# Pooled attention with a two-expert adapter: all gated activations of chunks 10 to 67 turned by DMA, in pairs

## The chip, the cores and the metric

The kernel runs on one core of one Trainium2 chip. The metric is the device time of one launch in microseconds (us). The kernel before was run three times: 378.42, 378.78 and 379.87, so its median is 378.78. Besides the five engines (PE for matrix products, DVE and ACT for elementwise work, POOL for more of it, SP for issuing transfers) the core has 16 DMA engines, which move data and can transpose 16-bit data on the way.

## The reference

`N` is 12288 queries for each of four batches, `C` is 128. Keys and values are the same 768 rows: 4 x 4 patches of `kv`, averaged and multiplied by `w_sr`. The attention output goes into a mixture of adapters with 8 experts of rank 16, of which the two with the largest logits count for each row.

```python
kv_pool = kv.reshape(B, H // r, r, W // r, r, C).mean(axis=(2, 4))
k = v = kv_pool.reshape(B, -1, C) @ w_sr
s = (q @ k.transpose(0, 2, 1)) / np.sqrt(C)
a = np.exp(s - s.max(-1, keepdims=True))
a /= a.sum(-1, keepdims=True) + 1e-09
x = (a @ v).reshape(B * N, C)                      # 49152 rows

logits = x @ w_gate
topk = the two largest of the 8 logits of each row
w = softmax over these two
out = x + sum over the two experts e of  w_e * (x @ A[e]) @ B[e]
```

## The kernel before, in words

The 49152 rows are 96 chunks of 512; a chunk is four tiles of 128 rows (`S` = 4). The main loop (line 588) has one slot per chunk, from slot 8 to slot 95; an order written out by hand (`opening`) stands in front of it and a tail behind it. Instructions run on each engine in the order in which the program gives them, and `keep` holds to that order.

In slot k, PE works on several chunks at once, each at another step:

- `unit()` three times (`scores`): two matmuls of 512 columns each give the scores of chunk k against a third of the keys, in one of two PSUM buffers (`ps_s`, tile `sg`); ACT writes their exponentials to `em`.
- `attend`, 24 matmuls: exponentials of chunk k-1 times the values (`acc`). The values carry a column of ones and seven differences of router logits, so that the sums and the logits come out of the same product.
- `normalize` (DVE, start of slot k, for chunk k-2): `xn` = `acc` / sum. `xn` tiles are a ring of six, two chunks to a tile. `top` (DVE) and `route`, `gates` (POOL, and a tanh on ACT) make the expert weights `gw`, two chunks at a time up to chunk 67.
- `transposes` (line 381): four PE transposes of `xn` of chunk k-4, and for some chunks four more of `hg` (below) of chunk k-5, into one PSUM tile `tt_ps`. One DVE copy brings it to SBUF (`tts`).
- `down` (line 427, chunk k-4): four matmuls with all experts' `A`, to `h_ps`. `gate` (line 432, DVE): `hg` = `h_ps` x `gw`, in bf16.
- `hg` must be transposed once more. For even chunks up to 60, and for 62 to 67, PE does this a slot later, within `transposes`. For odd chunks from 9 to 61 (`by_queue`, line 542) the gate writes to a tile `hs`, and `turn_h_dma` (line 422) has SP issue a DMA that transposes it into a tile `ht`.
- `up` (line 441): four matmuls with all experts' `B`, to `d_ps`; `finish` (line 450): DVE adds `xn` and writes `osb`, which SP stores. This comes two slots after the chunk's `down` where PE has transposed, six slots after it where the DMA has (`late_up`, line 677).

`tt_ps`, `d_ps` and `h_ps` take turns in two PSUM buffers (`ps_m`, tag `mb`). In the code of a slot the order is: first score unit, `transposes`, second unit (line 653), `up`, a quarter of `attend`, third unit, `down`, the other quarters.

From slot 72 on (chunks 68 to 89, `by_dma`) another branch of the loop runs (line 604): there both `xn` and `hg` are transposed by DMA, in tiles named `turn`, one transfer for both in a slot, and the order is first unit, `down`, second unit, `gate`, transfer, `up`, half of `attend`, third unit, the other half.

SP issues transfers in the order of the program: the stores, the loads of `kv` rows for the next batches (`load_kv`), the transposes, and `load_qT`, which loads 2048 queries by a transposing DMA from a bf16 copy in DRAM. `load_qT` stands in the slots of `loads` (line 481): every fourth slot from 10 to 62, and 57, 59, 61, 64, 65 and 66. In a slot with an odd chunk's DMA transpose it stands behind that transpose, otherwise at the start of the slot. POOL issues the casts to that copy.

Of the kernel before, what the change touches and what calls it, by code (L numbers as in the profile page):

```python
# [10 lines left out]
FP32 = mybir.dt.float32  # L11
BF16 = mybir.dt.bfloat16
# [8 lines left out]
def kernel(  # L21
# [10 lines left out]
    nc = tc.nc  # L32
    P = 128
    B, N, C = q.tensor.shape
# [5 lines left out]
    S = T // P  # L40
# [17 lines left out]
    gpool = ctx.enter_context(tc.tile_pool(name="gpool", bufs=6))  # L58
    run = ctx.enter_context(tc.tile_pool(name="run", bufs=3))
    hpool = ctx.enter_context(tc.tile_pool(name="hpool", bufs=4))  # L60
    opool = ctx.enter_context(tc.tile_pool(name="opool", bufs=8))
    qdram = ctx.enter_context(tc.tile_pool(name="qdram", bufs=1, space=bass.MemoryType.DRAM))
    ps_s = ctx.enter_context(tc.tile_pool(name="ps_s", bufs=2, space=bass.MemoryType.PSUM))
    ps_a = ctx.enter_context(tc.tile_pool(name="ps_a", bufs=1, space=bass.MemoryType.PSUM))
# [2 lines left out]
    keep = tc.keep_in_program_order  # L67
# [41 lines left out]
    q_f = {}  # L109

    def load_q(g, m):
        q_f[g, m] = opool.tile([P, S, C], FP32, tag="osb", name="qf")
        src = q[0, g * GT:(g + 1) * GT].rearrange("(p j) c -> p j c", p=P)
        keep(nc.sync.dma_start(q_f[g, m], src[:, m * S:(m + 1) * S]))

# [220 lines left out]
    SOLO, TURN = NCHUNK - 6, NCHUNK - 28  # L336
# [82 lines left out]
        for i, (d, k) in enumerate(what):  # L419
            d[k] = strip(t, 1)[:, lo + i]  # L420

    def turn_h_dma(k):
        hgT[k] = hpool.tile([P, S, P], BF16, tag="ht", name="ht", bufs=5)
        keep(nc.sync.dma_start(hgT[k].rearrange("c s p -> c s p"),
                               hg[k].rearrange("p s c -> p (s c)"), transpose=True))

    def down(k):
        hp[k] = mtile([P, S, P], name="h_ps")
# [3 lines left out]
    def gate(k, into=None):  # L432
        k0, m = first[k], k - first[k]
        hg[k] = run.tile([P, S, P], BF16, tag="hg", name="hg") if into is None else into
        keep(nc.vector.tensor_tensor(  # L435
            hg[k].rearrange("p s (e r) -> p (s e) r", e=E),
            hp[k].rearrange("p s (e r) -> p (s e) r", e=E),
            gw[k0][:, m * S:(m + 1) * S].rearrange("p s e -> p (s e)")
            .unsqueeze(2).broadcast_to([P, S * E, RK]), op=ALU.mult))
# [10 lines left out]
    def finish(k):  # L450
        osb = opool.tile([P, S, C], FP32, tag="osb", name="osb")
        keep(nc.vector.tensor_tensor(osb, dp[k], xn[k][:, :, 0:C], op=ALU.add))  # L452
        store(nc.sync, k, osb)
        for d in (em, acc, xn, xT, hgT, hp, hg, dp):
            d.pop(k, None)
# [19 lines left out]
    def unit(k=None, r=None):  # L475
        k, r = units.pop(0 if k is None else units.index((k, r)))
        scores(k, r)
# [61 lines left out]
        left = [k for k in left if k not in enter[t]]  # L539
        t += 1  # L540

    by_queue = [k for t in range(13, TURN - 2) for k in enter[t] if k % 2]
    late_up = {}

    kh, ku, kd, kdone = [], [], [], []
    engines = {"DVE": nc.vector, "ACT": nc.scalar, "POOL": nc.gpsimd}
# [41 lines left out]
    for k in range(k1, NCHUNK):  # L588
        b, i = divmod(k, NB)
        ka = att.get(k, [])  # L590
        kx = enter.get(k, [])
        begin(k, False)

        def after_norm(kn):
            top(kn)
            if kn == first[kn] + size[kn] - 1:
                route(first[kn])

        kn = [n for n in att.get(k - 1, []) if normed[n] == k]
        unit()  # L600
        if k in loads and not any(x_ in by_queue for x_ in kx):
            load_qT(loads[k])
        ku = ku + late_up.pop(k, [])
        if kx and not kd and all(x_ in by_dma for x_ in kx):
            down(kx[0])
            todo = []
            for n in kn:
                normalize(n)
                if n in by_dma:
                    narrow(n, k)  # L610
                    todo = [(xT, n)]
            tanhs()
            for h_ in kh:
                if h_ not in by_dma:
                    transposes(None, h_, nc.vector)
            unit()
            gate(kx[0], strip(k, 0)[:, 1])
            todo.append((hgT, kx[0]))
            if len(kx) == 1:
                turn_dma(k, *todo)  # L620
            for u_ in ku:
                up(u_)
                finish(u_)
            attend(ka[0], 0)
            attend(ka[0], 1)
            unit()
            for n in kn:
                after_norm(n)
            attend(ka[0], 2)
            for x_ in kx[1:]:  # L630
                down(x_)
                gate(x_, strip(k, 0)[:, 0])
                turn_dma(k, (hgT, x_), *todo)
            attend(ka[0], 3)
            kh, ku = kx, [c for c in kh if c not in by_queue]
            continue
        tanhs()
        for x_ in kd:
            down(x_)
        for n in kn:  # L640
            normalize(n)
            if n in by_dma:
                narrow(n, k)
                turn_dma(k, (xT, n))
        px = [c for c in kx if c not in by_dma]
        ph = [c for c in kh if c not in by_dma and c not in by_queue]
        pairs = [(px[j] if j < len(px) else None, ph[j] if j < len(ph) else None)
                 for j in range(max(len(px), len(ph)))]
        for x_, h_ in pairs[:1]:
            transposes(x_, h_, nc.vector)  # L650
        for x_ in kd:
            gate(x_)
        unit()
        for u_ in ku:
            up(u_)
            finish(u_)
        for a_ in ka[:-1]:
            for s in range(S):
                attend(a_, s)
            normalize(a_)  # L660
            after_norm(a_)
        if ka and len(ka) == 1:
            attend(ka[0], 0)
        for n in kn:
            after_norm(n)
        if k >= 13:
            unit()
            n0 = 1
        else:
            attend(ka[0], 1)  # L670
            n0 = 2
        for x_ in kx[:1]:
            down(x_)
            if x_ in by_queue:
                gate(x_, hpool.tile([P, S, P], BF16, tag="hs", name="hs"))
                turn_h_dma(x_)
                late_up[k + 6] = [x_]
                if k in loads:
                    load_qT(loads[k])
            else:  # L680
                gate(x_)
        kd = []
        if rest and i in ((14, 15, 16, 18, 19, 20, 21, 22, 23) if b == 0 else (5, 6, 7, 13, 14, 15, 21, 22, 23)):
            rest.pop(0)()
        for a_ in ka[-1:]:
            for s in range(n0 if len(ka) == 1 else 0, S):
                if s == S - 1:
                    for x_, h_ in pairs[1:]:
                        transposes(x_, h_, nc.scalar)
                        kd = [x_] if x_ is not None else []  # L690
                attend(a_, s)
        ku = [c for c in kh if c not in by_queue]
        kh = kx[:1] + kdone
        kdone = kd
        if k % 2 == 0 and 8 <= k <= 20:
            for _ in range(4 if k == 18 else 3):
                sums.pop(0)()
        for w in adds_at.get(k, []):
            add_patches(*w)
# [181 lines left out]
```

## Time and profile before

| | |
|---|---|
| median of the runs | 378.78 us (378.42 to 379.87) |
| the profiled execution | 378.59 us, of which the span from the first to the last instruction is 376.8 |
| stores of 256 KB | 94, median 4.0 us from issue to landing |
| DMA transposes into `ht` | 27, median 6.6 us |
| DMA transposes of the `turn` tiles | 23, median 3.1 us |
| query loads into `qT` | 18, median 8.1 us |

The profile is of one execution. The rows that the prediction quotes come from these views: the page (span, busy time of each engine, chain of waits); groups by tile (count, shortest, median and longest duration in ns, first and last start in us); the timeline (start in us, length in us, engine, line, operation, out<-in, count; in brackets the engine's idle time before, and who ended it); the waits of SP's queue (us in total, times, longest); and windows (for each engine busy us and instructions, then the granted clock of TensorE, the busy share of the 16 DMA engines and GB/s). L70 is a helper that issues all matmuls, so these are told apart by their tiles. The lengths of matmuls are modelled, their starts are recorded.

### The profile page before, as it was taken

The numbers are of one execution on the slowest core, as the hardware profiler recorded it, in microseconds if no ns is written. First come the engines' busy times: TensorE is split into PE (matmuls) and PEld (weight loads), VectorE is DVE, ScalarE is ACT, GpSimd is POOL, SyncE is SP. The second block draws the span as 40 slices with busy tenths as digits, with TensorE's granted clock in tenths as the row PEclk, the third lists the DMA queues.
The fourth block names the chain that finished last, engine by engine and source line by source line (L and its number), as shares of the span: only waits on it lengthen the run. The fifth ranks groups of instructions, "written<-read, shape, count | busy, mean of one in ns | idle before, by whom it ended". The sixth has DMA issues, their size and how long they took to land.

```text
span 376.8 us, 11335 instructions
## 1 busy us (share of the span) xinstructions
PE 365.9 (97%) x4340; PEld 287.5 (76%) x4340; DVE 300.5 (80%) x925; ACT 293.6 (78%) x368; POOL 218.2 (58%) x493
## 2 busy tenths in 40 slices
PE   8899999999999999999999999999999999999993
PEld 5667788877788787877877787787877777777782
DVE  1446799888888888888888888898898777777785
ACT  1548986787878788788878868877878999999873
POOL 0120368888766566557557566755645666666452
PEclk9999999999999999999999999999999999999997
DMA  8979669999999999999999999999875686777523
GB/s 255 397 261 218 231 176 271 298 268 255 240 288 265 185 288 312 182 241 294 240 259 249 287 275 203 204 257 243 211 211 156 169 170 170 169 151 186 143 88 139
DMA packets 66311, 85.75 MB, mean 228 GB/s; under 512 B 42736, under 2 KB 43504, under 8 KB 65904
## 3 DMA queue, kind: packets, MB, share of 16 engines
q1 hardware_dynamic: 62656, 73.29, 70.0%
q0 software_dynamic: 3168, 11.54, 18.2%
q8 instruction: 34, 0.56, 0.6%
q10 hardware_dynamic: 432, 0.20, 0.2%
q14 instruction: 21, 0.17, 0.2%
HBM read 50.53 MB, written 36.70 MB: 232 GB/s over the span
## 4 chain that ended last, share of the span: by engine, by line
PE 88%; DMA 6%; DVE 3%; ACT 1%; issue 1%; POOL 0%; SPq 0%; ACTq 0%; POOLq 0%
PE acc L70 35%; PE sg L70 32%; PE tt_ps L70 6%; PE d_ps L70 5%; PE h_ps L70 5%; DMA kvr<-in_kv_dram 4%; DMA qf<-in_q_dram 2%; PE v_ps L70 1%; PE kpT_ps L70 1%; DVE xn L330 1%; DVE tts L399 1%; DMA out_dram<-osb 1%; ACT em L304 1%; PE kfT_ps L70 0%; PE tail_ps L70 0%
## 5 line engine op out<-in xcount | busy, mean ns | idle before, releaser
L304 ACT ACTIVATE em<-sg 128x1024 f16<-128x1024 f32 x288 | 282.7, 1022 | 64.7 <-PE sg L70 62.0
L70 PE MATMUL acc<-vx,em 128*128 128x136 f16 x2280 | 166.5, 223 | 0.0
L70 PEld LDWEIGHTS <-em 128*128 128x128 f16 x2304 | 145.3, 98 | 8.2 <-DVE xn L330 0.6
L70 PE MATMUL sg<-qT,kfT 128*128 128x512 bf16 x480 | 142.0, 379 | 0.8 <-ACT em L304 0.7
L330 DVE TENSOR_TENSOR xn<-acc,rinv 128x540 f32<-128x540 f32 x95 | 68.4, 720 | 3.3
L452 DVE TENSOR_TENSOR osb<-d_ps,xn 128x512 f32<-128x512 f32 x91 | 62.4, 688 | 1.1
L362 POOL TENSOR_TENSOR over<-xn,srt 128x64 f32<-128x64 f32 (+1 forms) x120 | 30.9, 278 | 50.5 <-DVE srt L350 50.4
L502 POOL TENSOR_TENSOR kvr<-kvr 128x512 f32<-128x512 f32 (+1 forms) x48 | 56.9, 1201 | 0.5
L70 PEld LDWEIGHTS <-tts 128*128 128x128 bf16 x456 | 34.6, 97 | 25.4 <-issue 0.4
L70 PEld LDWEIGHTS <-kfT 128*128 128x128 bf16 x576 | 46.3, 98 | 4.5 <-issue 1.0
L377 POOL TENSOR_TENSOR gw<-th,over 128x64 f32<-128x64 f32 (+1 forms) x60 | 17.3, 289 | 51.7 <-ACT th L375 49.6
L325 DVE RECIPROCAL rinv<-acc 128x4 f32<-128x4 f32 x95 | 17.3, 182 | 36.1 <-PE acc L70 35.2
L399 DVE COPY tts<-tt_ps 128x1024 bf16<-128x1024 bf16 (+1 forms) x73 | 41.6, 569 | 0.0
L435 DVE TENSOR_TENSOR hg<-h_ps,gw 128x512 bf16<-128x512 f32 x44 | 30.4, 691 | 9.1 <-POOL gw L378 8.4
L70 PEld LDWEIGHTS <-xn 128*128 128x128 bf16 x296 | 22.6, 98 | 16.7 <-DVE xn L330 0.4
L350 DVE MAX8 srt<-xn 128x8 f32<-128x8 f32 x380 | 34.5, 153 | 0.1
L70 PE MATMUL sg<-qTs,kfT 128*128 128x512 bf16 x96 | 28.6, 379 | 0.0
L70 PE MATMUL tt_ps<-id_bf,xn 128*128 128x128 bf16 x284 | 27.4, 219 | 0.0
L70 PE MATMUL h_ps<-a_bf,tts 128*128 128x128 bf16 x284 | 27.4, 219 | 0.0
L368 POOL TENSOR_SCALAR over<-over 128x64 f32<-128x64 f32 (+1 forms) x60 | 19.8, 331 | 5.3
L225 POOL TENSOR_TENSOR kvr<-kvr 128x512 f32<-128x512 f32 x18 | 22.5, 1271 | 0.1
L70 PEld LDWEIGHTS <-turn 128*128 128x128 bf16 x176 | 13.4, 98 | 10.2 <-issue 0.2
(97 smaller groups left out, 318.4 us busy)
## 6 DMA issues: line engine op xcount, KB each, us to landing
out_dram<-osb SPq DMA_DIRECT2D x94, 256.0 KB, 4.0
kvr<-in_kv_dram SPq DMA_DIRECT2D x45, 512.0 KB, 6.5
qbf<-in_q_dram POOLq DMA_DIRECT2D x22, 512.0 KB, 8.1
qf<-in_q_dram SPq DMA_DIRECT2D x8, 256.0 KB, 7.6
kvr<-in_kv_dram SPq DMA_DIRECT2D x6, 256.0 KB, 7.6
ht<-hs SPq DMA_TRANSPOSE x27, 6.6
out_dram<-osb SPq DMA_DIRECT2D x3, 128.0 KB, 2.4
turn<-turn SPq DMA_TRANSPOSE x23, 3.1
```

The source lines that it names most:

```text
L70: return keep(nc.tensor.matmul(*a, **k))
L225: keep(adder.tensor_tensor(u[:, lo:hi], u[:, lo:hi], v[:, lo:hi], op=ALU.add))
L304: keep(nc.scalar.activation(o, i_, AF.Exp, bias=0.0, scale=scale))
L325: keep(nc.vector.reciprocal(ri, acc[k][:, :, VC]))
L330: keep(nc.vector.tensor_tensor(x[:, :, 0:VC], acc[k][:, :, 0:VC], ri.unsqueeze(2).broadcast_to([P, S, VC]), op=ALU.mult))
L350: keep(nc.vector.max(srt[k0][:, m, s], xn[k][:, s, C:C + E]))
L362: keep(eng.tensor_tensor(d, lg, so[:, :, i].unsqueeze(2).broadcast_to([P, n, 8]), op=ALU.subtract))
L368: keep(eng.tensor_scalar(mask, mask, 0.0, None, op0=ALU.is_ge))
L399: keep(nc.vector.tensor_copy(sb[:, lo:hi], ps[:, lo:hi]))
L435: keep(nc.vector.tensor_tensor(hg[k].rearrange("p s (e r) -> p (s e) r", e=E), hp[k].rearrange("p s (e r) -> p (s e) r", e=E), gw[k0][:, m ...
L452: keep(nc.vector.tensor_tensor(osb, dp[k], xn[k][:, :, 0:C], op=ALU.add))
L502: keep(nc.gpsimd.tensor_tensor(u, u, v, op=ALU.add))
```

## The change

`by_queue` becomes all chunks from 10 to 67. The gate writes two chunks, an even one and the odd one after it, into the halves of one `hs` tile, and after the odd one a single DMA transposes both into one `ht` tile (1024 columns instead of 512). Up-projections of these chunks come six slots after `down`, for chunks 62 to 67 four slots after it. Chunk 9 goes back to PE transposes. In the branch for all chunks before 72, `up` and `finish` now stand before the second score unit. `load_qT`, in slots whose chunk is in `by_queue`, stands at the end of that chunk's step as before; this now holds for even slots too. The output buffers `osb` shrink from eight to five, and four of the eight query tiles that are loaded at the start (those of g = 1) take the new `ht` buffers instead of output buffers; `hs` has three double buffers for four single ones, `ht` four double ones for five single ones.

```diff
@@ -58,7 +58,7 @@
-    opool = ctx.enter_context(tc.tile_pool(name="opool", bufs=8))
+    opool = ctx.enter_context(tc.tile_pool(name="opool", bufs=5))
@@ -109,7 +109,11 @@
     def load_q(g, m):
-        q_f[g, m] = opool.tile([P, S, C], FP32, tag="osb", name="qf")
+        if g:
+            t = hpool.tile([P, 2, S, P], BF16, tag="ht", name="qf")
+            q_f[g, m] = t.rearrange("p h s c -> p (h s c)").bitcast(FP32).rearrange("p (s c) -> p s c", s=S)
+        else:
+            q_f[g, m] = opool.tile([P, S, C], FP32, tag="osb", name="qf")
@@ -419,10 +423,11 @@
-    def turn_h_dma(k):
-        hgT[k] = hpool.tile([P, S, P], BF16, tag="ht", name="ht", bufs=5)
-        keep(nc.sync.dma_start(hgT[k].rearrange("c s p -> c s p"),
-                               hg[k].rearrange("p s c -> p (s c)"), transpose=True))
+    def turn_h_dma(k, strip_):
+        o = hpool.tile([P, 2, S, P], BF16, tag="ht", name="ht")
+        keep(nc.sync.dma_start(o.rearrange("c h s p -> c (h s) p"),
+                               strip_.rearrange("p h s c -> p (h s c)"), transpose=True))
+        hgT[k - 1], hgT[k] = o[:, 0], o[:, 1]
@@ -539,8 +544,8 @@
-    by_queue = [k for t in range(13, TURN - 2) for k in enter[t] if k % 2]
-    late_up = {}
+    by_queue = range(10, TURN)
+    late_up, pair = {}, []
@@ -611,7 +616,7 @@
             for h_ in kh:
-                if h_ not in by_dma:
+                if h_ not in by_dma and h_ not in by_queue:
                     transposes(None, h_, nc.vector)
@@ -650,10 +655,10 @@
-        unit()
         for u_ in ku:
             up(u_)
             finish(u_)
+        unit()
@@ -672,9 +677,12 @@
             if x_ in by_queue:
-                gate(x_, hpool.tile([P, S, P], BF16, tag="hs", name="hs"))
-                turn_h_dma(x_)
-                late_up[k + 6] = [x_]
+                if x_ % 2 == 0:
+                    pair = hpool.tile([P, 2, S, P], BF16, tag="hs", name="hs", bufs=3)
+                gate(x_, pair[:, x_ % 2])
+                if x_ % 2:
+                    turn_h_dma(x_, pair)
+                late_up.setdefault(k + (6 if x_ < 62 else 4), []).append(x_)
                 if k in loads:
                     load_qT(loads[k])
```

`TURN` is 68, and a chunk x from 2 on enters `down` in slot x + 4, up to chunk 67.

## The prediction

> **What bounds the kernel now.** I read the page first (busy time, DMA share, chain of waits), then the timeline of two ordinary slots, then SP's timeline, then the slots where the stages meet.
>
> ```profile
> span 376.8 us, 11335 instructions
> PE 365.9 (97%) x4340; PEld 287.5 (76%) x4340; DVE 300.5 (80%) x925; ACT 293.6 (78%) x368; POOL 218.2 (58%) x493
> ...
> PE 88%; DMA 6%; DVE 3%; ACT 1%; issue 1%; POOL 0%; SPq 0%; ACTq 0%; POOLq 0%
> ```
>
> PE is busy for 97% of the span and carries 88% of the chain. By these two lines every matmul taken away is time won. One level down it looks different. These are PE rows of slots 40 and 41 (start, length, operation), and ACT's exponentials in the same slots:
>
> ```profile
> 166.92 0.59 PE L70 MATMUL sg<-qT,kfT 128*128 128x512 bf16 x2
> 167.35 0.39 PE L70 MATMUL tt_ps<-id_bf,xn 128*128 128x128 bf16 x4
> ...
> 168.23 0.52 PE L70 MATMUL acc<-vx,em 128*128 128x136 f16 x6
> 168.69 0.59 PE L70 MATMUL sg<-qT,kfT 128*128 128x512 bf16 x2
> ...
> 170.40 0.59 PE L70 MATMUL sg<-qT,kfT 128*128 128x512 bf16 x2
> ...
> 171.06 0.39 PE L70 MATMUL tt_ps<-id_bf,hg 128*128 128x128 bf16 x4
> 171.28 0.59 PE L70 MATMUL sg<-qT,kfT 128*128 128x512 bf16 x2
> ...
> 172.29 0.59 PE L70 MATMUL sg<-qT,kfT 128*128 128x512 bf16 x2
> ...
> 174.01 0.59 PE L70 MATMUL sg<-qT,kfT 128*128 128x512 bf16 x2
> ```
>
> ```profile
> 167.61 1.02 ACT L304 ACTIVATE em<-sg 128x1024 f16<-128x1024 f32 x1 [0.86 <-PE sg L70]
> ...
> 171.09 2.85 ACT L304 ACTIVATE em<-sg 128x1024 f16<-128x1024 f32 x3 [0.49 <-PE sg L70]
> ```
>
> Starts tell more than lengths, because lengths are modelled. From one start to the next, a pair of score matmuls takes 0.43 us (166.92 to 167.35) and four transposes 0.22 (171.06 to 171.28). Slot 40 (no hg batch) lasts 3.48 (166.92 to 170.40), slot 41 (with one) 3.61 (170.40 to 174.01). The batch costs 0.22 but lengthens its slot by 0.13 only. In slot 40 six attention matmuls start at 168.23 and the third score unit at 168.69, 0.46 later, though six take 0.35 (eighteen take 1.06, 169.34 to 170.40 by the same reckoning). The 0.11 between is a wait: there are two score buffers, so the third unit needs the first unit's exponential out of the way. That one starts 0.69 after its unit (166.92 to 167.61) and lasts 1.02, to 168.63. So there is a floor: unit one to unit three at least 1.77, the rest of the slot 1.71, together 3.48, whatever PE has to do in between. By the busy line the change's 31 batches would be worth 31 x 0.22 = 6.8 (rival D); by the floor, half of that or less. The Trainium skill has a rule against the busy line: its page Perfetto Trace Analysis, section Identifying the Most-Contended Engine, calls matmul busy time no good measure of headroom and takes the weight loads' share instead, here 76%, by which the 6.8 is not promised. The trace agrees (the 0.11).
>
> The second thing under load is SP, which issues every transpose and store, in order. The tile rows for hs and ht, the late transposes of the turn strips, and SP's own timeline:
>
> ```profile
> L435 DVE TENSOR_TENSOR hs<-h_ps,gw x27: 690/692/692, 69.8 to 261.0; 128x512 bf16<-128x512 f32 x27
> L424 SPq DMA_TRANSPOSE ht<-hs x27: 1209/1292/2171, 70.5 to 268.3; - x27
> ...
> DMA to landing us min/median/max: 3.6/6.6/8.8
> ```
>
> ```profile
> L417 SPq DMA_TRANSPOSE turn<-turn x23: 1207/1232/2018, 280.6 to 353.2; - x23
> ...
> DMA to landing us min/median/max: 2.4/3.1/4.5
> ```
>
> ```profile
> 234.34 5.69 SPq L93 DMA_TRANSPOSE qTs<-qbf  x1
> ...
> 262.67 2.06 SPq L424 DMA_TRANSPOSE ht<-hs  x1
> ...
> 268.29 1.72 SPq L424 DMA_TRANSPOSE ht<-hs  x1
> 270.11 2.52 SPq L93 DMA_TRANSPOSE qTs<-qbf  x1
> 272.73 2.70 SPq L93 DMA_TRANSPOSE qT<-qbf  x1
> 275.52 2.82 SPq L448 DMA_DIRECT2D out_dram<-osb  x5
> ```
>
> The first hs was gated at 69.8 to 70.5 and issued at 70.5: no delay. The last was done at 261.7 and issued at 268.3: SP was 6.6 us late, behind the eight query loads of slots 57 to 66, and only at 278.3 (275.52 + 2.82) had it worked that off. Nobody waits for it today because chunk 61's up-projection comes only in slot 71.
>
> **The change, part by part.** Removed: the hg batches of 32 chunks (the even ones from 10 to 60, and 62 to 67), with one new one (chunk 9 in slot 14). A batch saves 0.13 where the slot has one up-projection. Those are the odd slots 19 to 67 and slot 68: 26 x 0.13 = -3.4. Slots 15 and 17 have a batch and no up-projection now; they are at the floor already: 0. Slot 14: +0.13. DVE's copies shrink to half, but DVE is not on the path: 0. Slots 16 to 19 lose their up-projections (0.22 of PE each) because these now come six slots after entering; they stay at the floor, so this wins nothing, and the four return where slots are full: 70, 71, 74 and 75 get two each.
>
> The up-projection in front of the second score unit: its input was finished in an earlier slot, and the span from unit one to unit three is the same sum in another order. In ordinary slots 0.
>
> It does cost where a slot has two, as 69 and 71 do today. All small PE results share two PSUM buffers, so the second up-projection takes the transposes' buffer and waits for DVE to copy it:
>
> ```profile
> 272.52 0.59 PE L70 MATMUL sg<-qT,kfT 128*128 128x512 bf16 x2
> ...
> 273.60 0.69 DVE L399 COPY tts<-tt_ps 128x1024 bf16<-128x1024 bf16 x1
> ...
> 274.34 0.38 PE L70 MATMUL d_ps<-b_bf,ht 128*128 128x128 bf16 x4
> ...
> 277.00 0.59 PE L70 MATMUL sg<-qT,kfT 128*128 128x512 bf16 x2
> ...
> 279.04 0.59 PE L70 MATMUL sg<-qT,kfT 128*128 128x512 bf16 x2
> ...
> 281.27 0.59 PE L70 MATMUL sg<-qT,kfT 128*128 128x512 bf16 x2
> ...
> 285.52 0.59 PE L70 MATMUL sg<-qT,kfT 128*128 128x512 bf16 x2
> ...
> 289.15 0.59 PE L70 MATMUL sg<-qT,kfT 128*128 128x512 bf16 x2
> ...
> 292.32 0.59 PE L70 MATMUL sg<-qT,kfT 128*128 128x512 bf16 x2
> ```
>
> Slot 69 lasts 4.48 (272.52 to 277.00), slots 70 to 73 last 4.27, 4.25, 3.63 and 3.17. The copy in slot 69 starts 1.08 after the slot does; a half copy (halves of the same row: about 0.41) would end at 1.49, so in the new order the second up-projection starts at about 1.53 instead of at 0.87 (0.43 + 0.22 + 0.22): a stall of 0.66 with no score unit to cover it. Unit one to unit three becomes 1.53 + 0.22 + 0.43 + 0.35 = 2.53. Slot 70 had 2.04 (277.00 to 279.04): +0.49. Slot 71, double in both versions, should have had the 2.39 of slot 69 (272.52 to 274.34, plus 0.22 and 0.35): +0.14. Slot 69 itself, single in the change, goes from 2.39 to the floor's 1.77: -0.62. Slot 72 loses its lone hg batch and its copy and should look like slot 73: -0.47.
>
> In the last stage the second one waits for the gate:
>
> ```profile
> 299.70 0.68 DVE L435 TENSOR_TENSOR turn<-h_ps,gw 128x512 bf16<-128x512 f32 x1
> ...
> 299.95 0.87 PE L70 MATMUL acc<-vx,em 128*128 128x136 f16 x12
> ```
>
> The gate ends at 300.38, so a second up-projection would run from 300.44 to 300.66 and attention would start 0.71 later than 299.95. Slots 74 and 75: +1.42.
>
> Sum on PE alone: -3.4 + 0.13 - 0.62 + 0.49 + 0.14 - 0.47 + 1.42 = -2.3.
>
> Now the transposes. SP issues 29 instead of 27. A transpose of 1024 columns takes SP no longer than one of 512 (1232 against 1292 ns): 0 on SP, hidden as before. DMA engines move 31 batches more; priced below. Transposes now wait for the odd chunk of a pair, so an even chunk has five slots instead of six from issue to use: 17.4 us, against 6.6 of landing and a usual delay of a few us. Hidden. But chunks 62 to 67 have four, and 62 has only from the end of slot 67 to early in slot 70, while SP is late. That is the term that decides. Queue order in the change: transpose 60/61, the query loads of slots 65 and 66, a store each, then transpose 62/63. Today's rows put the last query load at 272.73 to 275.43. With a store of 0.56 (2.82 / 5) the pair's transpose is issued at 276.0. Landing: between 3.1 (the turn strips' median, same size, quieter) and 6.6 (ht's median); I take 4.4, near the turn strips' largest, since the load in front of it is still moving. It lands at 280.4. PE would get there at 277.00 less what it has won since slot 57 (six slots at 0.13, and 0.62) = 275.6, plus 1.53 = 277.1. Stall: 3.3. SP itself will be later too: five double transposes stand in this stretch, and where the queue is crowded one takes SP 1.72 to 2.06 instead of 1.21. If doubling the bytes doubles that excess, each adds 0.5 to 0.85, up to 4 in all, or 0 if the engines have room (the kv, store and load rows do not change). I take 1.5. Stall 4.8, bounds 2 (landing of 3.1, no crowding) to 9.5 (6.6 and 4).
>
> Query loads at even slots now go behind that slot's store: 0.56 later, and six slots (20.9) pass before first use, against a delay of 6.6 and a landing of up to 8.8: 0. Output buffers 8 to 5: a buffer has five slots (17.4) from add to reuse; a landing of up to 8.8, and up to two query loads ahead (5.69 and 2.5), make 17.0: at the edge between slots 58 and 66; 0, at most 2. The two g=1 query tiles' new place is read out long before slot 15: 0.
>
> Profiled execution: 378.59 (span 376.8, 1.8 around it); it lies 0.2 below the median of the runs, 378.78. 378.59 - 2.3 + 4.8 = **381.1**.
>
> **Rivals.**
> *A, it lands in time* (the other side). If SP is no later than PE, the stall is absent and -2.3 stays: 376.3. For it: landings in the late stage take 3.1, and SP was without delay at the beginning. Against: 268.3 behind 261.7. It decides from a landing before 277.1, 3.3 us earlier than the 280.4 of today's rows. Chance 0.2.
>
> *B, DMA engines become the bound long before slot 57.* A round of four slots in the middle, the late stage, and one store-only microsecond of the tail:
>
> ```profile
> 195.80:210.10 14.30, 14.30 (x182) 11.34 (x180) 12.31 (x38) 11.71 (x15) 9.76 (x19) 1.00 1.14 255
> ...
> 300.00:330.00 30.00, 30.00 (x367) 23.39 (x364) 22.65 (x78) 28.94 (x40) 20.09 (x68) 1.00 0.71 165
> 372.00:373.00 1.00, 0.37 (x2) 0.21 (x2) 0.54 (x3) 0.02 (x1) 0.00 (x0) 0.50 1.03 389
> ```
>
> The DMA share is 1.14 in the middle. In the late stage a slot of 3.17 holds one store and one transpose of 1024 in 0.71 x 3.17 = 2.25 us; the store is 0.67 (256 KB at 389 GB/s), the transpose 1.57, a batch of 512 columns 0.78. The change adds one per two slots: +0.11 of share. If 1.14 is full, 26 batches make SP 20 us late by slot 57; the margin of an even chunk (17.4 - 6.6 - 1.3, about 9.5) takes half, and some 8 to 10 us more reach PE beside the 3.3: 387 to 390. Against it stands a row of SP's waits:
>
> ```profile
> SPq L424 <- DVE rinv L325: 15.0, 12, 1.9
> ```
>
> Twelve of the 27 issues stood waiting for DVE, so SP was on time for them. Chance 0.18.
>
> *C, the clock.* The last window row has a granted clock of 0.50, in a microsecond where PE is busy for 0.37; a stall of 4.8 could do that in mid-kernel. At half clock the dense half of a slot (1.71) doubles, two at most: 382.8 to 384.5. The Trainium skill has a rule for this (TensorE: Matmul & The Clock Gate, section HAM oscillation — how this bites in real kernels: an idle gap beyond about 3.4 us re-throttles PE). By that rule the forecast's own stall would halve the clock for a window; the tail's 0.50 agrees, but no row shows it in mid-kernel. Chance 0.12.
>
> *D, PE is bound after all,* each batch worth 0.22: 31 x 0.22 = 6.8, at best 371.8. Against: the 3.48 floor. Chance 0.05.
>
> My forecast (stall of 1.5 to 8, 377.8 to 384.3): 0.45.
>
> **Numbers.** 0.5% (1.9 us) is what can be told from no change. Faster: A, mostly, and D: 0.22. Same: the small stalls of my own case and a little of A: 0.18. Slower: 0.60. The range leaves out D and the end of B: 375.8 to 388; the forecast's own is 377.8 to 384.3.
>
> **What would show it.** PE slots 20 to 60 all at 3.48 apart from those with key work (right), or odd ones at 3.39 or less (D). In slot 70 a PE gap before the up-projection of chunk 62, ended by the DMA into ht (right), or none (A). Waits of PE for ht before slot 60, or of SP's delay growing round by round (B). A granted clock below 1.00 after slot 70 (C). Slots 74 and 75 near 3.9. I am wrong if slot 70 waits less than 1 us.

## The result: 390.4 us, 2.8% slower, and the profile after

The changed kernel takes 390.38 us (median of four runs, 387.91 to 405.36), the kernel before 378.99 beside it: ratio 1.0278, 95% interval 1.0238 to 1.0318. The forecast was 381.1 with a range of 375.8 to 388.0, so the sign was right and the size was outside the range. Executions of the changed kernel, and of most variants below whose DMA engines are overloaded, scatter by 8 us and more where the kernel before stays within 6, so medians stand with their ranges, ratios are of the executions within 1.5% of their kernel's fastest, and the readings rest on the one profiled execution of each kernel.

The profiled execution took 389.96 us. Its page (span, PE's busy time, the granted clock and the DMA engines in 40 slices, the chain of waits):

```profile
span 388.0 us, 11056 instructions
PE 364.6 (94%) x4210; PEld 282.5 (73%) x4216; DVE 287.3 (74%) x924; ACT 294.9 (76%) x368; POOL 218.7 (56%) x493
...
PEclk9999999999999999999999999999959999999997
DMA  7989589989999999999999999899995977677523
...
PE 79%; DMA 12%; DVE 3%; ACT 1%; issue 1%; SPq 1%; POOL 1%; POOLq 0%; DVEq 0%; ACTq 0%
```

PE has 130 instructions less on record, but its busy time fell by 1.3 us only, and PE's share of the chain fell from 88% to 79% while DMA's doubled to 12%. A single slice of the clock row has a 5. The waits of PE in the changed kernel (us in total, times, longest) name the transfer:

```profile
PE d_ps L70 <- DMA ht<-hs: 10.4, 4, 8.3
```

Slot lengths, here and below, are the intervals between the starts of consecutive reciprocals (`rinv`), one per slot. In ordinary slots the change did what the forecast said. Starts of the first score units of slots 40 to 42, in the timeline of the changed kernel:

```profile
165.38 0.59 PE L70 MATMUL sg<-qT,kfT 128*128 128x512 bf16 x2
...
168.86 0.59 PE L70 MATMUL sg<-qT,kfT 128*128 128x512 bf16 x2
...
172.34 0.59 PE L70 MATMUL sg<-qT,kfT 128*128 128x512 bf16 x2
```

Both slots last 3.48 (168.86 - 165.38, 172.34 - 168.86): the odd one lost 0.13 of its 3.61, the even one stayed at the floor. Then slot 70, PE's timeline and the two reciprocals at its ends:

```profile
276.19 0.59 PE L70 MATMUL sg<-qT,kfT 128*128 128x512 bf16 x2
...
276.85 0.39 PE L70 MATMUL d_ps<-b_bf,ht 128*128 128x128 bf16 x4
285.50 0.61 PE L70 MATMUL d_ps<-b_bf,ht 128*128 128x128 bf16 x4 [8.26 <-DMA ht<-hs]
285.90 1.06 PE L70 MATMUL sg<-qT,kfT 128*128 128x512 bf16 x2
...
291.09 0.59 PE L70 MATMUL sg<-qT,kfT 128*128 128x512 bf16 x2
```

```profile
276.39 0.18 DVE L329 RECIPROCAL rinv<-acc 128x4 f32<-128x4 f32 x1 [0.27 <-PE acc L70]
...
291.29 0.18 DVE L329 RECIPROCAL rinv<-acc 128x4 f32<-128x4 f32 x1 [0.55 <-PE acc L70]
```

The slot lasts 14.90 instead of 4.27, 10.6 more. PE waits 8.26 for chunk 62's half of `ht`, in the place the forecast named. The score matmuls behind the wait are listed at 1.06 instead of 0.59, and the window from 285.50 to 289.00 has a granted clock of 0.50 with PE busy throughout:

```profile
285.50:289.00 3.50, 3.50 (x19) 2.40 (x20) 0.97 (x5) 1.50 (x2) 0.99 (x4) 0.50 1.15 229
```

The Trainium skill (TensorE: Matmul & The Clock Gate, section HAM oscillation — how this bites in real kernels) says that an idle gap beyond about 3.4 us throttles PE again; this trace agrees, with 8.26 us of gap and 0.50 behind it. Another trace does not put the boundary there: in before_dram (below) the clock was 0.50 in the 3 us behind a gap of 2.66 us (183.10) and 1.00 behind one of 3.42 (300.34).

Why the pair came so late is in the timelines of DVE and SP. The first two rows are the gates of chunk 53 in slot 57, which ends at 231.37 (230.68 + 0.69), and of chunk 63 in slot 67, which ends at 268.38; the others are SP's:

```profile
230.68 0.69 DVE L440 TENSOR_TENSOR hs<-h_ps,gw 128x512 bf16<-128x512 f32 x1 [0.27 <-PE h_ps L70]
...
267.69 0.69 DVE L440 TENSOR_TENSOR hs<-h_ps,gw 128x512 bf16<-128x512 f32 x1 [0.27 <-PE h_ps L70]
```

```profile
235.78 1.53 SPq L428 DMA_TRANSPOSE ht<-hs  x1
237.41 5.17 SPq L93 DMA_TRANSPOSE qTs<-qbf  x1
...
278.02 2.61 SPq L93 DMA_TRANSPOSE qT<-qbf  x1
...
281.34 1.32 SPq L428 DMA_TRANSPOSE ht<-hs  x1
```

In the kernel before SP issued that chunk's transpose at 232.40, 0.03 us after its gate; here it is 4.4 late (235.78 - 231.37) before the eight query loads begin. At the pair 62/63 it issues at 281.34, 13.0 behind the gate, where the forecast had 276.0. All differences of slot length add up to 11.7 us: -2.0 for the small terms (their sizes are below; +0.43 of slot 94, which the forecast did not have, is in it), +3.6 in five waits in slots 52, 54, 56, 64 and 68 that the forecast did not have either, and +10.1 in slot 70 beyond its planned +0.49.

### The profile page after: what moved, and what is told of

Read it like the earlier page. It is cut to its first block, busy times and chain, and to the rows that moved or that the text cites. A ratio compares the mean times of both kernels' runs of the same rounds, so it can differ in the third digit from the quotient of the medians.

```text
span 388.0 us, 11056 instructions
## 1 busy us (share of the span) xinstructions
PE 364.6 (94%) x4210; PEld 282.5 (73%) x4216; DVE 287.3 (74%) x924; ACT 294.9 (76%) x368; POOL 218.7 (56%) x493
## 4 chain that ended last, share of the span: by engine, by line
PE 79%; DMA 12%; DVE 3%; ACT 1%; issue 1%; SPq 1%; POOL 1%; POOLq 0%; DVEq 0%; ACTq 0%
PE acc L70 32%; PE sg L70 29%; DMA ht<-hs 7%; PE d_ps L70 5%; PE h_ps L70 5%; PE tt_ps L70 4%; DMA kvr<-in_kv_dram 3%; PE kpT_ps L70 2%; PE v_ps L70 1%; DMA out_dram<-osb 1%; ACT em L308 1%; DVE xn L334 1%; SPq L93 1%; DVE tts L403 1%; DVE kvr L141 1%
## 5 line engine op out<-in xcount | busy, mean ns | idle before, releaser
L308 ACT ACTIVATE em<-sg 128x1024 f16<-128x1024 f32 x288 | 283.1, 1024 | 74.5 <-PE sg L70 69.1
L70 PEld LDWEIGHTS <-em 128*128 128x128 f16 x2304 | 148.2, 98 | 24.9 <-DVE xn L334 12.1
L440 DVE TENSOR_TENSOR hs<-h_ps,gw 128x512 bf16<-128x512 f32 x58 | 40.1, 692 | 24.2 <-POOL gw L382 11.5
L70 PEld LDWEIGHTS <-kfT 128*128 128x128 bf16 x576 | 47.3, 98 | 6.1 <-issue 1.5
L70 PEld LDWEIGHTS <-tts 128*128 128x128 bf16 x332 | 24.8, 98 | 16.0 <-issue 0.5
L70 PE MATMUL d_ps<-b_bf,ht 128*128 128x128 bf16 x232 | 22.7, 221 | 12.5 <-DMA ht<-hs 10.4
L403 DVE COPY tts<-tt_ps 128x512 bf16<-128x512 bf16 (+1 forms) x72 | 32.9, 457 | 0.0
L70 PEld LDWEIGHTS <-ht 128*128 128x128 bf16 x232 | 15.4, 98 | 14.4 <-DMA ht<-hs 12.4
```

What stands on the lines that cost most here:

```text
L70: return keep(nc.tensor.matmul(*a, **k))
L308: keep(nc.scalar.activation(o, i_, AF.Exp, bias=0.0, scale=scale))
L403: keep(nc.vector.tensor_copy(sb[:, lo:hi], ps[:, lo:hi]))
L440: keep(nc.vector.tensor_tensor(hg[k].rearrange("p s (e r) -> p (s e) r", e=E), hp[k].rearrange("p s (e r) -> p (s e) r", e=E), gw[k0][:, m ...
```

## The experiments

Three questions: what fills slot 70, whether the DMA engines are the bound, and whether the rest of the forecast (the floor, the order, the buffers) holds.

**Query loads out of the way (late_loads).** Only the late query loads move:

```diff
-    loads.update({57: 20, 59: 21, 61: 22, 64: 18, 65: 23, 66: 19})
+    loads.update({64: 18, 66: 19, 72: 20, 76: 21, 80: 22, 84: 23})
```

> The changed kernel with the query loads of groups 20 to 23 issued in slots 72, 76, 80 and 84 instead of 57, 59, 61 and 65. Theory (SP and the DMA engines are full from about slot 45 on, and the four loads that crowd slots 57 to 66 keep the transpose of chunks 62 and 63 waiting): SP works its delay off before slot 67, slot 70 falls from 14.9 to about 4.8, no lower clock, the small waits of slots 52 to 56 stay; 378.3, from 377 to 380. Rival (the doubled transposes alone keep the DMA engines full, whatever else is queued): slot 70 stays above 10, 387 or more.

Measured: ratio 1.0093 (1.0045 to 1.014), median of all ten executions 388.24 (380.28 to 409.92). In the profiled execution (388.80) slot 70 is 0.49 longer than before, exactly the planned term: with the loads gone no stall is left there. PE's rows:

```profile
281.49 0.59 PE L70 MATMUL sg<-qT,kfT 128*128 128x512 bf16 x2
...
283.01 0.38 PE L70 MATMUL d_ps<-b_bf,ht 128*128 128x128 bf16 x4 [0.48 <-DVE tts L403]
...
286.25 0.59 PE L70 MATMUL sg<-qT,kfT 128*128 128x512 bf16 x2
```

Chunk 62's up-projection starts 1.52 behind the slot's first score unit (the forecast's 1.53), after 0.48 of waiting for DVE's copy, and the next slot begins 3.24 after it. By the ratio two thirds of the loss came back; in many executions, the profiled one among them, it did not. In that one the moved loads cost 3.7 more in slots 74, 82 and 86, and a greater loss sits 55 us earlier than slot 70, in slot 54 (+8.6). SP's queue, and PE:

```profile
201.49 6.15 SPq L428 DMA_TRANSPOSE ht<-hs  x1
...
210.13 15.39 SPq L93 DMA_TRANSPOSE qT<-qbf  x1
```

```profile
222.41 0.61 PE L70 MATMUL d_ps<-b_bf,ht 128*128 128x128 bf16 x4 [6.19 <-DMA ht<-hs]
```

```profile
202.00:222.00 20.00, 14.22 (x172) 10.94 (x168) 12.26 (x39) 12.81 (x16) 12.34 (x22) 0.96 1.27 144
```

One transpose holds SP for 6.15 us, one query load for 15.39; the window between shows the DMA share at 1.27 and only 144 GB/s, where 250 is usual. In this execution, then, there is trouble before the stretch of query loads too.

**Spin in the wait (spin_70).** 36 matmuls on zeros in front of chunk 62's up-projection, so that PE does not idle:

```diff
         for u_ in ku:
+            if u_ == 62:
+                spin(36)
             up(u_)
```

> The changed kernel with 36 matmuls of 512 columns of zeros (7.8 us of PE work) in front of the up-projection of chunk 62, so that PE is busy in place of waiting. Theory (about 2.3 us of slot 70 are PE at half clock after the wait of 8.3): granted clock 1.00 there, slot 70 about 12.6, 387.7. Rival (what follows the wait is slow for another reason, such as DVE or ACT that have to catch up): slot 70 stays at 14.9 or grows, 390 or more.

Measured: 394.1 (one run). PE's rows of slot 70 and the window behind the spin:

```profile
283.41 8.39 PE L70 MATMUL spin_ps<-zero 128*128 128x512 bf16 x36
291.64 0.38 PE L70 MATMUL d_ps<-b_bf,ht 128*128 128x128 bf16 x4
```

```profile
290.50:296.00 5.50, 5.42 (x56) 3.91 (x55) 3.22 (x11) 2.36 (x3) 0.99 (x4) 1.00 1.01 212
```

The spin fills 8.23 us (291.64 - 283.41), as long as the wait, and the clock behind it is 1.00. The slot lasts 13.0, 8.72 longer than before: the planned 0.49 and the spin's 8.23, and nothing behind them. In the changed kernel chunk 62's up-projection starts 9.31 behind the slot's first score unit (285.50 - 276.19), 7.79 later than in late_loads, and the next slot begins 5.59 after it (291.09 - 285.50) instead of 3.24. So of slot 70's 10.1, 7.8 are the late transfer and 2.3 the low clock behind it; the 8.26 in the row holds 0.48 of waiting for the copy that was planned. The total of spin_70 is higher because of other waits (slot 46 +4.2).

**The loads' place in even slots (load_first).** The query loads of even slots go back to the start of the slot:

```diff
-        if k in loads and not any(x_ in by_queue for x_ in kx):
+        if k in loads and not any(x_ in by_queue and x_ % 2 for x_ in kx):
...
-                if k in loads:
+                if k in loads and x_ % 2:
```

> The changed kernel with the query loads of even slots back at the start of the slot, in front of that slot's store. Theory (their place in the queue does not matter): SP's delay at slot 57 stays at 2 to 6 us, slot 70 at 13 to 16, 388 to 392. Rival (the loads' new place behind the store makes the queue late): delay at slot 57 below 1, slot 70 shorter by 4 or more, 386 or less.

Measured: 392.78 (one run), slot 70 +9.2, and waits in slots 52 (+2.4) and 54 (+1.8). Putting the loads back did not remove the stall, so their place is not the cause.

**Chunks 62 to 67 by PE again (after_62_pe).** `by_queue = range(10, 62)`.

> The changed kernel, but chunks 62 to 67 turned by PE again (26 instead of 29 transposes by DMA, up-projections of 62 on as before). The forecast's account (one stall in slot 70, elsewhere the slots as forecast) gives 390.4 less the 10.6 of slot 70 less about 0.7 of slots 74 and 75: 379. Theory of full DMA engines: the same stall is gone, but the waits of PE for ht in slots 52 to 68 stay (2.3 us and scattered), or move, so 380 to 386 with more scatter than the kernel before has.

Measured: median 399.5 (389.5 to 402.25). The forecast's account, one stall in one place, gives 379 and falls: even the fastest execution is 10 above it. The pair that was late is gone, and in the profiled execution (397.18) PE's weight loads wait 9.5 us for `ht` in five other places, DVE 4.6 for a store once; slots 54, 64 and 69 are 5.2, 5.3 and 5.7 longer.

**More DMA work in the kernel before (before_double, before_plain).** PE's work is that of before. In before_double each transpose of `ht` has 1024 columns, of which the second half is zeros and not used; in before_plain a plain load of 256 KB into a spare tile follows each:

```diff
+        keep(nc.sync.dma_start(plain[k // 2 % 3], q[0, 0:GT].rearrange("(p j) c -> p j c", p=P)[:, 0:S]))
```

> The kernel before, with each DMA transpose of an odd chunk widened from 512 to 1024 columns; the second half is constant zeros and nobody reads it. The same PE work and the same place in SP's queue as before; output, hs and ht buffers as in the changed kernel. Theory (the bytes of the transposes make SP late): SP's delay at the transpose of slot 57 grows from 0.03 us to 3 or more, and in slots 59 to 65 from 6 to 8 to 10 or more; up-projections six slots on hide most, 378.5 to 384. Rival (SP is late because of the faster slots or the new order, not because of the bytes): delays as before, at most 1 at slot 57, 378.6.

> The kernel before with a plain load of 256 KB (2 KB packets) into a spare tile behind each of its 27 transposes of ht, and 5 output buffers; nobody reads the loads. In the kernel with doubled transposes 27 second halves cost 18 us. If any extra work on full engines does this: SP's delay grows from 7 to 10 us at slot 57 and beyond, PE waits for ht, 385 to 400 us with scatter. Rival (it is the 256-byte packets of transposes that do not go together with the casts): 378.6 to 380, SP's delay at slot 57 under 3 us.

Measured: 397.31 (one run), and median 399.84 (393.54 to 401.99). It does not take transposes: 27 plain loads of 256 KB cost about as much as the 27 second halves of 128 KB. But both kernels had five output buffers, as the changed one has, and the waits of before_plain show another operand in the front:

```profile
DVE osb L454 <- DMA out_dram<-osb: 21.4, 10, 4.1
```

**Five buffers alone, and extra work with eight (before_o5, before_dram).** `bufs=8` to `bufs=5` and nothing else; and, with eight, a copy of 256 KB from DRAM to DRAM behind each transpose:

```diff
+        keep(nc.sync.dma_start(plain[k // 2 % 3], q[0, 0:T]))
```

> The kernel before with five output buffers instead of eight, nothing else. Forecast (0, at most 2 between slots 58 and 66, where SP is late): 378.5 to 380.5, no wait of DVE for a store before slot 57. Rival (five are too few in any case): DVE waits for stores all over the middle, 383 or more.

> The kernel before, all eight output buffers, with a copy of 256 KB from DRAM to DRAM behind each of its 27 transposes of ht; nobody reads the copies. Theory (engines that are full hold PE up by whatever is late first): SP's delay over 4 us at slot 57 and over 10 after it, waits of PE for ht, queries or stores of 3 us and more, 382 to 400. Rival (only the five buffers turned the extra work into a loss): SP is late too, but 378.5 to 380.5.

Measured: before_o5 379.06 (378.36 to 385.8), ratio 1.0029 (1.0001 to 1.0056), in the profiled execution all slots as before. As long as nothing is late, three buffers less cost 0.3%, below the 0.5% that can be told from no change. before_dram: median 386.53 (384.08 to 392.9), ratio 1.0185 (1.0151 to 1.022). The waits of its profiled execution (392.9, the longest of the four):

```profile
PEld L70 <- DMA ht<-hs: 7.6, 4, 3.2
...
PEld L70 <- DMA turn<-turn: 4.3, 2, 3.9
...
PEld L70 <- DMA qT<-qbf: 3.2, 3, 2.6
```

In the kernel before with extra work, whatever has the least slack comes late: stores' buffers where there are five, `ht`, `turn` and queries where there are eight. So the bound isn't found in the operand that waits, but in what all of them share.

**Room made on the engines (after_thin, before_thin, after_nocast, after_thin_nocast).** Thin: the stores of chunks 10 to 59 write half of their columns, the other half is left out. Nocast: 14 of the casts are left out, and the loads of their queries read the copy of group 7 instead.

```diff
-        store(nc.sync, k, osb)
+        if 10 <= k < 60:
+            store(nc.sync, k, osb[:, 0:2], 0, 2)
+        else:
+            store(nc.sync, k, osb)
```

```diff
     def cast_q(g):
+        if 8 <= g <= 21:
+            q_bf[g] = q_bf[7]
+            return
```

> The changed kernel, but chunks 10 to 59 store only half of their columns (128 KB instead of 256 KB each), so that the DMA engines get back about 0.33 us per slot of the 0.39 that the doubled transposes add; PE, DVE, ACT and the order of SP's issues are as in the changed kernel. Theory (the DMA engines are full in the middle and their backlog is what makes SP late and the transposes land late): SP's delay at slot 57 is back under 1 us, no PE wait for ht before slot 68, slot 70 at most 5 us longer than before instead of 10.6, and 377 to 382 us in all. Rival (SP's order alone, its queue of issues, makes the transposes late): waits and time stay as in the changed kernel, 388 to 392.

> Control: the kernel before with the same half stores of chunks 10 to 59. Theory (the kernel before just fits into the DMA engines; no wait of PE is theirs in the middle): 378 to 379 us, all slots up to 67 within 0.02 of before, SP's delay after slot 57 shorter than its 6.6. Rival (the kernel before is already held up by full engines): 377 or less.

> The changed kernel without the 14 casts of query groups 8 to 21 (512 KB of bf16 each, issued by POOL in slots 20 to 57); the loads of these groups read group 7's cast instead, so all transposes, loads and stores of SP are as in the changed kernel. Theory (the engines have no room for the doubled transposes, whoever takes the room): the casts hold the engines for about as much as half of all transposes and loads, so without them SP is on time at slot 57, no PE wait for ht before slot 62, slot 70 at most 3 us longer than before, 375 to 379 us and all runs within 2 us of each other. Rival (the transposes hold up each other, casts or not): stalls in slots 52 to 70 and a scatter of 5 us or more stay, 385 to 395.

> The changed kernel with both reliefs at once: chunks 10 to 59 store half of their columns, and the casts of query groups 8 to 21 are left out (their loads read group 7's). Theory (room on the DMA engines decides both the scatter and slot 70): odd slots 0.12 shorter, no PE wait for ht before slot 70, slot 70 at most 1.5 us longer than before, 376 to 377.5 us, all runs within 1 us of each other. Rival (something else than room makes the scatter): runs of 385 us and more among them.

Measured: before_thin 378.31, ratio 0.9981 (0.9955 to 1.0008): the kernel before is not held up by its stores. (Its SP delay behind slot 57 was 7.4 to 8.9, not below 6.6 as expected: half stores alone do not relieve that stretch.) The profiled execution of after_thin took 376.84 us, and there everything is as forecast for a transpose in time: slots 19 to 67 sum to -3.2, no wait for `ht` up to slot 69, slot 70 +1.05. Its transposes of chunks 52/53 and 62/63:

```profile
229.63 1.28 SPq L428 DMA_TRANSPOSE ht<-hs  x1
...
271.58 1.25 SPq L428 DMA_TRANSPOSE ht<-hs  x1
```

The pair is issued at 271.58 instead of 281.34. The kernel's other three executions took 386.7 to 391.0; that isn't explained, since there is a trace of the one only.

after_nocast: 385.57 (384.14 to 386.07), ratio 1.0162 (1.0119 to 1.0205). The scatter is gone, and so are all waits up to slot 67. Slot 70 is still 9.1 longer. The gate of chunk 53, SP's rows and PE's wait:

```profile
229.20 0.69 DVE L443 TENSOR_TENSOR hs<-h_ps,gw 128x512 bf16<-128x512 f32 x1 [0.27 <-PE h_ps L70]
```

```profile
229.92 2.03 SPq L431 DMA_TRANSPOSE ht<-hs  x1
232.04 5.55 SPq L96 DMA_TRANSPOSE qTs<-qbf  x1
...
277.95 1.32 SPq L431 DMA_TRANSPOSE ht<-hs  x1
```

```profile
281.41 0.61 PE L70 MATMUL d_ps<-b_bf,ht 128*128 128x128 bf16 x4 [6.49 <-DMA ht<-hs]
```

SP is on time at slot 57 (0.03 behind the gate) and 12.4 late ten slots later, behind the loads. This separates the two parts of the loss: the casts against the doubled transposes in the middle (3.6 us in slots 52 to 68, SP 4.4 late, the scatter), and the stretch of query loads, which by itself costs a wait of 6.5 plus the clock. What was expected of slot 57 and of the waits before slot 62 held; that slot 70 would be at most 3 longer, and 375 to 379 us, did not. With both reliefs (after_thin_nocast) the ratio is 1.0017 (0.9971 to 1.0062), the median 381.47 (376.84 to 384.44): in the profiled execution the pair is issued at 273.00 and PE waits 2.6. The fastest run comes within 0.6 of the forecast's rival A, but the scatter of 1 us that was expected is 8: the stretch of loads remains at the edge.

The Trainium skill (Perfetto Trace Analysis, section What "DMA-bound" means) lists full DMA engines and a solid issuing queue as two different bounds. SP's queue is solid behind slot 57, so by that page the sequencer would be a candidate. The grouped rows of 18 query loads on SP, of the changed kernel and of after_nocast (shortest, median and longest in ns), speak for the engines:

```profile
L93 SPq DMA_TRANSPOSE qT<-qbf x18: 2552/3981/6933, 31.3 to 278.0; - x18
```

```profile
L96 SPq DMA_TRANSPOSE qT<-qbf x18: 1505/2720/5816, 32.1 to 274.5; - x18
```

The same 18 instructions take SP 3981 ns in the median and only 2720 where POOL's casts are left out. But most of them stand before the stretch in question, and the median says nothing of lateness (in the kernel before it is 4520). Behind slot 57 it looks different. Lateness is the time from the end of a pair's gate to its issue; before and before_thin have chunks 53 and 61 in place of the pairs:

| profiled execution | late at 52/53 | at 60/61 | at 62/63 | SP's time for the eight query loads of slots 57 to 66 |
|---|---|---|---|---|
| before | 0.03 | 6.65 | - | 26.2 |
| before_thin | 0.03 | 7.41 | - | 26.2 |
| changed | 4.42 | 10.61 | 12.96 | 28.2 |
| after_nocast | 0.03 | 10.32 | 12.37 | 31.8 |
| after_thin_nocast | 0.03 | 5.46 | 7.38 | 25.6 |

The window from 232 to 276 us of before, of the changed kernel, of after_nocast and of after_thin_nocast:

```profile
232.00:276.00 44.00, 43.87 (x542) 34.77 (x540) 38.27 (x114) 35.12 (x43) 25.41 (x50) 1.00 0.96 220
232.00:276.00 44.00, 42.38 (x510) 33.05 (x509) 35.01 (x112) 35.32 (x42) 25.31 (x49) 1.00 1.07 254
232.00:276.00 44.00, 42.06 (x506) 32.81 (x504) 35.39 (x114) 35.13 (x42) 25.64 (x49) 1.00 1.04 219
232.00:276.00 44.00, 42.02 (x506) 32.82 (x504) 35.34 (x114) 35.08 (x42) 26.27 (x52) 1.00 0.97 206
```

Leaving out the casts does not help here: SP begins on time and is nearly as late ten slots later. So the lateness at 62/63 is not brought along from the middle; the stretch makes it. Halving the stores does help: the eight loads take SP 6.2 us less, the DMA share falls from 1.04 to 0.97 and SP is 5.0 less late, with the same issues in the same order. So engines without room hold SP here too, for some 6 us of the eight loads' time. The other 26 are there in the kernel before, with whole and with half stores alike; for them room on the engines changed nothing, and the queue itself stays a candidate. This rests on one trace of each.

**The order of up-projection and second unit alone (before_up_first).** The diff's reordering, in the kernel before.

> The kernel before with the up-projection put in front of the second score unit, nothing else. Forecast's terms: 0 in ordinary slots, +0.14 in each of slots 69 and 71 (two up-projections): 378.9, not to be told from before. Rival (the score unit behind it comes 0.22 later, and the exponential with it, in every slot): 60 x 0.1 to 0.2, 385 to 391.

Measured: 379.26, ratio 1.002 (1.0003 to 1.0037). Ordinary slots do not move (medians of even and odd slots 0.00), SP is 6.6 late at chunk 61 as before, slots 69 and 71 cost +0.30 and +0.41, and slot 94 +0.43, which nobody had expected.

**The floor (before_down).** In the kernel before, `down` moves in front of the third score unit from slot 13 on:

```diff
         if k >= 13:
+            for x_ in kx[:1]:
+                down(x_)
             unit()
             n0 = 1
...
         for x_ in kx[:1]:
-            down(x_)
+            if k < 13:
+                down(x_)
```

> The kernel before, with the down-projection put in front of the third score unit from slot 13 on; nothing else. Theory of the forecast (unit one to unit three is a floor of 1.77 set by the first exponential and the two score buffers, and 0.11 of it is PE waiting): four down matmuls (0.22) fill that wait, so slots without an hg batch go from 3.48 to about 3.39 and slots with one stay at 3.61: 24 x 0.09 = 2.2 less, 376.6 in all. Rival (PE is not waiting there, the starts only look so): all slots as before, 378.8. Second rival (the down matmuls wait for DVE's copy when they stand earlier): slots longer by 0.1 or more, 381 or more.

Measured: 376.16 (375.2 to 383.57), ratio 0.9918 (0.9877 to 0.9959): faster than both kernels. PE's rows of slot 40:

```profile
165.98 0.60 PE L70 MATMUL sg<-qT,kfT 128*128 128x512 bf16 x2
...
167.65 0.39 PE L70 MATMUL h_ps<-a_bf,tts 128*128 128x128 bf16 x4
167.87 0.60 PE L70 MATMUL sg<-qT,kfT 128*128 128x512 bf16 x2
...
169.37 0.59 PE L70 MATMUL sg<-qT,kfT 128*128 128x512 bf16 x2
```

`down` starts at 167.65 where PE used to wait for the exponential, and the slot lasts 3.39 (169.37 - 165.98) instead of 3.48; odd slots from 19 on are unchanged except slot 21 (+0.11). The 0.11 of waiting that the forecast read from starts is real, and it can be had without any transfer.

## Why the prediction was right on PE and wrong on the DMA side

**The floor and the small terms: right.** Odd slots 0.12 to 0.13 shorter, four with key work 0.17 to 0.18, not 0.22 (rival D is dead); slots 19 to 67 -3.2 where nothing is late. Slot 14 +0.12 (forecast +0.13), 69 -0.77 (-0.62), 70 +0.49 without the stall (+0.49), 71 +0.11 (+0.14), 72 -0.47 (-0.47), 74 and 75 +0.70 each (+0.71). Together -2.4, forecast -2.3. Slot 94's +0.43 was missing; with it -2.0.

**Edits at nothing: right.** The order in ordinary slots (before_up_first), the loads' place (load_first) and five buffers (before_o5) cost nothing that counts, though the buffers are the first to give way where stores are late (before_plain).

**The stall in slot 70: right place, wrong size.** The forecast had PE ready for chunk 62 at 277.1 and a stall of 3.3 + 1.5 = 4.8. PE would have been ready at 277.71 (276.19 + 1.52), and the stall was 7.8. The landing is not to blame: 4.4 in the forecast, and 4.2 from the issue to PE's start (281.34 to 285.50). The term that failed is the issue, "the pair's transpose is issued at 276.0", with its 1.5 for crowding: it came at 281.34, 5.3 later. In the forecast's own terms 3.3 + 5.3 - 0.2 - 0.6 = 7.8. Of the 5.3, 3.1 were there when the first query load was issued (237.41 against 234.34 before), but after_nocast, with SP on time at that point, is 12.4 late at the pair all the same. So what was priced too low is the stretch itself: in the kernel before, SP falls 6.6 behind in it by chunk 61, and the forecast went on from there; in the changed kernel the engines have less room (share 1.07 against 0.96), and in after_nocast SP falls 10.3 behind by the same point. The stall lies inside the bounds of 2 to 9.5.

**The clock: rival C was a part of the same case, not another.** The low clock cost 2.3 behind the stall, inside C's price of 1.7 to 3.4, and the forecast's own case had no term for it. It also followed the 6.49 of idle time in after_nocast, and not the 2.61 in after_thin_nocast, where the next slot begins 3.26 after the up-projection.

**Rival B was put aside on the wrong row.** "Twelve of the 27 issues stood waiting for DVE, so SP was on time for them" is true and says only that no backlog was left over from one round of four slots to the next. It says nothing of how much more fits in. The DMA share of 1.14, which the forecast quoted, was the warning. The window from 90 to 245 us of before, of the changed kernel, of before_double and of after_nocast:

```profile
90.00:245.00 155.00, 155.00 (x1909) 123.43 (x1907) 135.08 (x406) 123.81 (x149) 101.03 (x188) 1.00 1.05 250
```

```profile
90.00:245.00 155.00, 153.44 (x1832) 119.80 (x1832) 125.88 (x409) 125.13 (x150) 101.54 (x190) 1.00 1.08 260
```

```profile
90.00:245.00 155.00, 145.48 (x1722) 114.43 (x1720) 121.25 (x368) 112.23 (x134) 92.14 (x171) 0.97 1.08 241
```

```profile
90.00:245.00 155.00, 154.96 (x1853) 121.04 (x1852) 126.92 (x413) 125.61 (x151) 94.84 (x178) 1.00 0.92 220
```

The share is the second last number. It goes from 1.05 to 1.08 and not much further, however much is asked (1.09 in before_dram, 1.10 in load_first), while the slots grow. (after_thin's profiled execution has 1.08 too and before_o5's 1.07, both without such waits: the share says that there's little room left, and SP's delay whether it is used up.) B's size was also wrong: SP was 4.4 late at slot 57, not 20. Its delay does not only grow: it was 10.7 at the pair 46/47 (issued at 218.55) and came down again. B's total of 387 to 390 holds the profiled 389.96 by a different split: 3.6 in the middle and 10.1 in slot 70, of which after_nocast shows 8.6 without any help from the middle.

The accounting in one line: 378.59 - 2.0 + 3.6 + 7.8 + 2.3 = 390.3, against 389.96 for the profiled execution (rounding of some ninety slots, and the stretch outside them).

Open: why a single transpose issued at 201 to 204 us holds SP for 6 to 11 us in the changed kernel, late_loads and after_62_pe (7.0, 6.15 and 11.4), near the casts of slots 49 and 51, and why after_thin's other runs were long. Fewer casts remove such waits; which packets collide isn't shown. Nor is it shown what holds SP for 26 us of the eight query loads even where the stores are halved, or separated what in the changed kernel makes the stretch of query loads worse than before: the order alone (before_up_first) and five buffers alone (before_o5) leave SP 6.6 and 6.2 late at chunk 61, but the doubled transposes and the shorter slots were not tried apart there.

## What to carry to other kernels

Before moving work to the DMA engines, ask how much more fits in, not whether the queue is on time today: a queue that was just on time at a share of 1.05 had little in reserve here, and the overload came out at whichever operand had the least slack. Cost a late operand with everything that follows it: the wait, the delay that the issuing queue gathers in the stretch in front of it, and the clock behind a long idle gap. And where starts show an engine waiting a tenth of a microsecond per slot at a fixed point, move some of its own work into that gap first; here that was worth 0.8% and needed no transfer.

## What the runs showed of the hardware that was not expected

- The busy share of the 16 DMA engines, from 90 to 245 us, is 1.07 to 1.10 in every overloaded kernel, with transposes, plain loads and DRAM copies alike (short windows go higher, as the 1.27 below); what grows instead is the time for which SP is held by an issue (1.2 us for a transpose at rest, 7.0 at most in the changed kernel, 15.39 for a query load in late_loads).
- Overload makes the time itself uncertain: 380.28 to 409.92 in late_loads, against 377.82 to 381.84 for the kernel before on the same chip; without the casts 384.14 to 386.07.
- Moved bytes can fall while the engines look busier: 144 GB/s at a share of 1.27 (late_loads, 202 to 222 us).
- A low clock follows shorter gaps than expected, but not always: 0.50 behind 2.66 us of idle PE and 1.00 behind 3.42 (both before_dram), 0.56 behind 2.83 (before_plain, 264.41), 1.00 behind 2.61 (after_thin_nocast).
